# Constant products in TensorE's waits, a shorter table build, two output queues and a moved conversion schedule in a recurrence-plus-experts kernel

## The chip, the core and the metric

The kernel runs on one core of one Trainium2 chip. The core has TensorE (PE in the profile; PEld is its weight load), VectorE (DVE), ScalarE (ACT), GpSimd (POOL) and SyncE (SP), which issues transfers. ScalarE and GpSimd can issue transfers as well, each on a queue of its own. The metric is device microseconds of one execution, as the median of several runs.

## What is computed

Three stages in a row, all f32, with B=4, H=8, S=768, D=48 and 3072 tokens of width 384:

```python
for t in range(S):                               # decayed linear attention
    cur = einsum('bhd,bhe->bhde', u * k[t], v[t])
    y[t] = einsum('bhd,bhde->bhe', r[t], state + cur)
    state = w * state + einsum('bhd,bhe->bhde', k[t], v[t])
x = y.reshape(tokens, 384)
x = max(x @ w1, x @ w2, x @ w3) @ w_out          # 384 -> 768 -> 384
xn = x / sqrt(mean(x * x) + 1e-6) * rms_g
out = (silu(xn @ w_gate) * (xn @ w_val)) @ w_out2   # 384 -> 1536 -> 384
```

## The kernel before

Tokens go in 24 tiles of 128 (six chunks of time, four batches); a **unit** is the four tiles of a chunk, 512 tokens, and units are numbered from 0. The recurrence is done chunk-wise: `raw` (r and k, transposed) is multiplied by tables of powers of `w` and of their reciprocals (`qk`, made by `tables`), TensorE multiplies the two (**scores**, `pe_a`, tile `pa`), VectorE puts them under a mask into `Dg`, and TensorE forms the **output** `py` (`pe_y`) and the **state product** `pkv` (`pe_st`). `tables2` and `tables3` make another table, `kt`, which TensorE transposes (tile `pk`). ScalarE and VectorE split each output into a high and a low part, `x`.

Every large product is done as three (`mm3`, L99 to L101: high by high, high by low, low by high). In the first expert stage (`a_l1`) a unit has 18 **slots**, six blocks f by three weights w, of nine products each, and then six slots of output products (`a_out`). A slot's result `pl{unit}_{f}_{w}` takes one of four PSUM banks (`psm`) in turn; w=0 is copied out by ScalarE (`c`), w=1 and w=2 are maximised into it by VectorE, and after w=2 ScalarE casts the result to `h1h`. So slot 9 is f=3, w=0, and slot 13, f=4, w=1, takes the bank that slot 9 had. The four `psx` banks hold `pa`, `py`, `pkv` and `pk`.

Weights come as 64-bit words. A **conversion** (`tick`) of one piece is a load (`wraw`, SP), three ScalarE activations (`conv_exp`, L137 to L140), one VectorE operation a tick later, and then the split into high and low (unit 0's weights) or weight sums on VectorE and a store to HBM. It needs a `wf` buffer of six, which the store of six pieces earlier has to give back. In unit 0 ticks follow the table `U0T`; in units 1 to 4 there are nine, behind the slots n for which n % 8 is 0, 3 or 6.

The order on each engine is the order of the code: `att_steps` gives the recurrence in steps, and the loop over slots takes so many of them after each slot. Before anything else TensorE multiplies a constant by itself 24 times (`WARM`, L634). Its products are plain f32 of 128x128 by 128x128, and each leaves two records in the trace. The second expert stage (units two at a time) is not touched but for the last transfers, in `b_out`: for the last unit ScalarE or VectorE copies each finished third into SBUF, the last third in two halves, and SP transfers the four pieces (L939, L943).

Of the kernel before, what the change touches and what calls it, by code (L numbers as in the profile page):

```python
# [9 lines left out]
F32 = mybir.dt.float32  # L10
# [6 lines left out]
ALU = mybir.AluOpType  # L17
# [9 lines left out]
NRU = 8  # L27
DVE_WL = (2, 16, 19, 22)
RMS_EARLY = 2
WARM = 24  # L30
TKI = (0, 0, 2)
TKP = (1, 1, 1, 1, 1, 1)
HF = 2
# [27 lines left out]
NB = S // 128  # L61
NT = B * NB
NP = H // 2
# [3 lines left out]
def r32(ap):  # L67
    return ap.bitcast(F32)
# [3 lines left out]
def rwkv_moe_kernel(ctx, tc, rkT, rkv, wd, ub, cst, rg, w1p, wo1p, w2p, out):  # L72
    nc = tc.nc
    act, dve, pool, pe, sync = nc.scalar, nc.vector, nc.gpsimd, nc.tensor, nc.sync
# [7 lines left out]
    ap_ = sA.enter_context(tc.tile_pool(name="moea", bufs=1, side="left"))  # L82
    tp = sT.enter_context(tc.tile_pool(name="att", bufs=1, side="right"))
# [10 lines left out]
    ones = cp.tile([128, 128], F32R, name="ones")  # L94
# [3 lines left out]
    def mm3(o, lh, ll, rh, rl, start, stop, **kw):  # L98
        pe.matmul(o, lh, rh, start=start, stop=False, **kw)  # L99
        pe.matmul(o, lh, rl, start=False, stop=False, **kw)  # L100
        pe.matmul(o, ll, rh, start=False, stop=stop, **kw)  # L101
# [119 lines left out]
    def tick(n=1):  # L221
        for _ in range(n):
            i = tick_n[0]
            tick_n[0] += 1
            for off, fn in ((3, conv_load), (1, conv_exp), (0, conv_shift), (-1, conv_put)):
                if 0 <= i + off < NJ:
                    fn(i + off)
# [3 lines left out]
    ident = cp.tile([128, 128], F32, tag="wf", bufs=6, name="ident")  # L231
    cmask = csb[:, 0:128].bitcast(U32)
    m01 = csb[:, 128:129], csb[:, 130:131]
    small = tp.tile([128, 4, NP], F32, name="small")
    wsb, wcl, w128, ok = (small[:, n] for n in range(4))
    usb = tp.tile([128, DM], F32, name="usb")
    qk = tp.tile([128, 2, NP, 128], F32, name="qk")
    kt = tp.tile([128, DM], F32, name="kt")
# [22 lines left out]
        loads.append(lambda: sync.dma_start(t[:, VO:], rkv[i, :, 2 * DM:]))  # L261

    def tables():
        p = ap_.tile([128, NP, 65], F32, tag="h1h", name="ptab")
        pool.memset(p[:, :, 0:1], 1.0)
        dve.tensor_scalar(out=wcl, in0=wsb, scalar1=0.7, scalar2=1.1, op0=ALU.max, op1=ALU.min)
        dve.tensor_tensor(out=ok, in0=wsb, in1=wcl, op=ALU.is_equal)
        dve.tensor_copy(p[:, :, 1:2], wcl.unsqueeze(2))
        n = 1
        while n < 64:  # L270
            dve.tensor_tensor(out=p[:, :, n + 1:2 * n + 1], in0=p[:, :, 1:n + 1],
                              in1=p[:, :, n:n + 1].to_broadcast([128, NP, n]), op=ALU.mult)
            n *= 2
        dve.reciprocal(qk[:, 1, :, 64:128], p[:, :, 1:65])
        act.copy(qk[:, 0, :, 64:128], p[:, :, 0:64])
        act.copy(qk[:, 1, :, 0:64], p[:, :, 63::-1])
        act.copy(qk[:, 0, :, 0:64], qk[:, 1, :, 127:63:-1])
        return p

    def tables2(p):  # L280
        w64 = p[:, :, 64:65]
        dve.tensor_tensor(out=w128.unsqueeze(2), in0=w64, in1=w64, op=ALU.mult)
        R = ap_.tile([128, NP, 128], F32, tag="c1", bufs=3, name="Rtab")
        dve.tensor_tensor(out=R[:, :, 64:128], in0=qk[:, 1, :, 0:64],
                          in1=w64.to_broadcast([128, NP, 64]), op=ALU.mult)
        dve.tensor_tensor(out=R[:, :, 0:64], in0=qk[:, 1, :, 0:64],
                          in1=w128.unsqueeze(2).to_broadcast([128, NP, 64]), op=ALU.mult)
        return R

    def tables3(R):  # L290
        pk = psx.tile([128, NP, 2, 64], F32, tag="x", name="pk")
        for pr in range(NP):
            pe.transpose(pk[:, pr].rearrange("p j d -> p (j d)"), R[:, pr, :], ident)
        act.copy(kt.rearrange("p (r j d) -> p r j d", j=2, d=D), pk[:, :, :, 0:D])
# [45 lines left out]
    def prep2(i):  # L340
        if i // B < NB - 1:
            k = st[i]["tm"][:, KO:KO + DM]
            pool.tensor_tensor(out=k, in0=k, in1=kt, op=ALU.mult)

    def pe_a(i):
        s = st[i]
        raw = s["raw"]
        pa = [psx.tile([128, NP, 128], F32, tag="x", name=f"pa{i}_{j}") for j in range(2)]
        for pr in range(NP):
            for j in range(2):  # L350
                sl = slice(64 * j, 64 * j + 48)
                pe.matmul(pa[j][:, pr], raw[sl, 1, pr], raw[sl, 0, pr], start=True, stop=True)  # L352
        s["pa"] = pa
# [50 lines left out]
    def pe_y(i):  # L404
        s = st[i]
        c, b = divmod(i, B)
        tm = s["tm"]
        py = s["py"] = psx.tile([128, 3, 128], F32, tag="x", name=f"py{i}")
        lanes = []
        for n in range(4):  # L410
            lane = []
            for k in range(3):
                m = (n + TURN[k] * (i >= TURNED)) % 4
                pr, o = (k, 32 * m) if m < 3 else (3, 32 * k)
                ops = [(tm[:, VO + 144 * pr + 48 * j + o:VO + 144 * pr + 48 * j + o + 32],
                        s["Dg"][:, 2 * pr + j]) for j in range(2) if o != (64, 0)[j]]
                if c > 0:
                    ops.append((Tst[b][:, pr, o:o + 32], s["raw"][:, 0, pr]))
                for m, (l, r) in enumerate(ops):
                    lane.append((py[32 * n:32 * n + 32, k], l, r, m == 0, m == len(ops) - 1))  # L420
            lanes.append(lane)
        for m in range(max(map(len, lanes))):
            for lane in lanes:
                if m < len(lane):
                    o, l, r, start, stop = lane[m]
                    pe.matmul(o, l, r, start=start, stop=stop)  # L426
# [84 lines left out]
    def a_l1(u, f, w, o=0, n=512):  # L511
        cs = slice(o, o + n)
        xh, xl = xt[u][:, 0], xt[u][:, 1]
        if u not in hs:
            if u == NB - 1:
                t = sB["r"].tile([128, 2, F1, 512], F32R, tag="h2", name=f"h1{u}")
                hs[u] = t[:, 0], t[:, 1]
            else:
                hs[u] = [ap_.tile([128, F1, 512], F32R, tag=t, name=f"{t}{u}") for t in ("h1h", "h1l")]
        hh, hl = (t[:, f, cs] for t in hs[u])  # L520
        p = psm.tile([128, 512], F32, tag="m", name=f"pl{u}_{f}_{w}_{o}")
        wt = wts["a", f]
        for k in range(3):
            sl = slice((w * 3 + k) * 128, (w * 3 + k) * 128 + 128)
            mm3(p[:, :n], wt[:, 0, sl], wt[:, 1, sl], xh[:, k, cs], xl[:, k, cs], k == 0, k == 2)
        if w == 0:
            c1 = ap_.tile([128, 512], F32, tag="c1", bufs=3, name=f"c1{u}_{f}_{o}")
            a_l1.c1 = c1
            act.copy(c1[:, :n], p[:, :n])  # L529
        else:  # L530
            c1 = a_l1.c1
            dve.tensor_tensor(out=c1[:, :n], in0=p[:, :n], in1=c1[:, :n], op=ALU.max)  # L532
        if w == 2:
            act.copy(hh, c1[:, :n])  # L534
            later.append(lambda: (pool if n < 512 else dve).tensor_tensor(
                out=hl, in0=c1[:, :n], in1=r32(hh), op=ALU.subtract))
# [77 lines left out]
    with tc.manual_schedule():  # L614
        pool.memset(wsb, 1.0)
        dve.memset(raws[0], 0.0)
        for j in range(2):
            sync.dma_start(wsb[64 * j:64 * j + 48], wd[48 * j:48 * j + 48])
        load_tile(0)
        load_next(4)  # L620
        sync.dma_start(ident, cst[:, 0:128])
# [10 lines left out]
        pw = psm.tile([128, 512], F32, tag="m", name="pw")  # L632
        for _ in range(WARM):
            pe.matmul(pw[:, 0:128], r32(ones), r32(ones), start=True, stop=True)  # L634
        steps = list(att_steps())
        pos = 0
        tick(TKI[0])
        tb = tables()
        load_tile(1)
        load_next(4)  # L640

        prep(0)
        pe_a(0)
        tick(TKI[1])
        prep_b(0)
# [174 lines left out]
        for u in range(NB):  # L820
# [14 lines left out]
            for n, sl in enumerate(slots):  # L835
# [25 lines left out]
                if u == 0:  # L861
                    tick(U0T[n] if n < len(U0T) else 0)
                elif u < L:
                    if n % 8 in (0, 3, 6):
                        tick()
                elif u == L:
                    if n == 0:
# [62 lines left out]
        def b_out(f, d, h, po, first, last, u):  # L930
            wt = wo[f]
            o = 128 * d
            mm3(po[d], wt[:, 0, o:o + 128], wt[:, 1, o:o + 128], h[0], h[1], first, last)
            if not last:
                return
            ob = sb.pop(0) if d == 2 else br.tile([128, 512], F32, tag="ob", bufs=2, name=f"ob{u}_{d}")
            if u < NB - 1 or d < 2:
                (dve.tensor_copy if d == 1 else act.copy)(ob, po[d])
                sync.dma_start(out[u, :, d], ob)  # L939
            else:  # L940
                for eng, cs in ((act.copy, slice(0, 256)), (dve.tensor_copy, slice(256, 512))):
                    eng(ob[:, cs], po[d][:, cs])
                    sync.dma_start(out[u, :, d, cs], ob[:, cs])  # L943
            if d == 2:
                sb.append(ob)

# [53 lines left out]
        for p in range(NB // 2):  # L1000
# [84 lines left out]
            last_m, n = {}, 0  # L1085
# [11 lines left out]
            n = 0  # L1097
            for m, (_, _, kind, g, arg) in enumerate(plan):
                if kind == "M":
# [26 lines left out]
                    f = n // 10 + 2  # L1126
# [30 lines left out]
            for b in range(3 * F2 - (9 if more else 0)):  # L1157
                f, d = divmod(b, 3)
# [194 lines left out]
```

## Time and profile before

| | us |
|---|---|
| median of 3 runs (lowest, highest) | 810.82 (810.12, 811.65) |
| the profiled execution | 817.82 |
| its span, first to last instruction | 816.1 |
| TensorE busy in the span | 792.5 (97%) |
| VectorE, ScalarE, GpSimd busy | 570.2, 418.7, 210.3 |

The span is what the trace shows; the profiled execution has 1.7 us around it, and it is 0.9% longer than the median of the unprofiled runs. A busy TensorE is not one at its peak: its clock is granted at one of two levels, 1.0 (2.4 GHz) or 0.5 (1.2 GHz), and the mean over the span is 0.986. In the view of windows the clock stands behind the busy times.

### The profile page before, as it was taken

The page shows a single profiled execution, that of the slowest core. Times are in us where ns is not written, and L with a number is a line of the kernel's source. Part 1 is how long each engine was busy: PE and PEld are TensorE (multiplying, and loading weights), DVE is VectorE, ACT ScalarE, POOL GpSimd, SP SyncE. Part 2 cuts the span into 40 slices and gives each one's busy share as a digit, 9 for nine tenths or more (in the row PEclk, how much of TensorE's full clock was granted, in tenths as well). Part 3 has the DMA queues.
Part 4 walks back from the last instruction along what each step waited for, and adds up shares of the span by engine and source line. Part 5 has one row for each costly group of instructions (what it writes and reads, how often), then busy time and mean ns, then how long its engine had stood idle before and what let it go on. Part 6 is the DMA issues. An engine that isn't in the chain of part 4 may idle for free.

```text
span 816.1 us, 14059 instructions
## 1 busy us (share of the span) xinstructions
PE 792.5 (97%) x5098; PEld 654.7 (80%) x5098; DVE 570.2 (70%) x980; ACT 418.7 (51%) x780; POOL 210.3 (26%) x225
## 2 busy tenths in 40 slices
PE   6799999999999999999999999999999999999996
PEld 6688888778888888888888888788888788888884
DVE  8888859759968758518947679866677974665551
ACT  1888773444454453223577666555444555444431
POOL 2376633424325313012457673000000000000000
PEclk8889999999999999999999999999999999999998
DMA  8976775676577653226269874318454405554211
GB/s 243 262 220 202 244 223 143 217 220 196 154 243 206 196 184 104 75 86 203 87 216 345 292 237 162 129 52 278 137 182 152 124 32 173 156 155 139 74 40 43
DMA packets 83738, 139.28 MB, mean 171 GB/s; under 512 B 10566, under 2 KB 47046, under 8 KB 83660
## 3 DMA queue, kind: packets, MB, share of 16 engines
q1 hardware_dynamic: 80316, 122.37, 49.5%
q0 software_dynamic: 3200, 15.73, 5.0%
q8 instruction: 42, 0.69, 0.4%
q14 instruction: 36, 0.29, 0.1%
q10 hardware_dynamic: 144, 0.20, 0.1%
HBM read 98.65 MB, written 35.41 MB: 164 GB/s over the span
## 4 chain that ended last, share of the span: by engine, by line
PE 87%; DVE 5%; DMA 3%; ACT 2%; issue 1%; POOL 0%; SPq 0%; DVEq 0%; ACTq 0%; POOLq 0%
PE px L99 11%; PE px L100 11%; PE px L101 11%; PE pl L99 8%; PE pl L101 8%; PE pl L100 8%; PE pa L100 5%; PE pa L101 5%; PE pa L99 5%; PE py L426 4%; PE pa L352 3%; PE po L99 3%; PE po L100 3%; PE po L101 3%; PE pkv L390 1%
## 5 line engine op out<-in xcount | busy, mean ns | idle before, releaser
L99 PE MATMUL pl<-x,w_a 128*128 128x512 f32 (+1 forms) x342 | 131.9, 386 | 2.0 <-ACT c L529 1.9
L101 PE MATMUL pl<-x,w_a 128*128 128x512 f32 (+1 forms) x342 | 129.6, 379 | 1.3 <-DVE w_a L156 0.7
L100 PE MATMUL pl<-x,w_a 128*128 128x512 f32 (+1 forms) x342 | 129.5, 379 | 0.2 <-DVE x L442 0.2
L99 PEld LDWEIGHTS pl<-x,w_a 128*128 128x128 f32 x342 | 64.3, 188 | 15.7 <-ACT c L529 2.3
L532 DVE TENSOR_TENSOR c<-pl,c 128x512 f32<-128x512 f32 (+1 forms) x76 | 50.0, 657 | 37.6 <-PE pl L101 31.7
L101 PEld LDWEIGHTS pl<-x,w_a 128*128 128x128 f32 x342 | 64.3, 188 | 14.0 <-DVE w_a L156 0.9
L100 PEld LDWEIGHTS pl<-x,w_a 128*128 128x128 f32 x342 | 64.3, 188 | 11.9 <-DVE x L442 0.4
L1071 DVE TENSOR_TENSOR px<-px,sb 128x512 f32<-128x512 f32 x56 | 39.0, 699 | 33.1 <-PE px L101 31.5
L335 POOL TENSOR_SCALAR_AFFINE_SELECT Dg<-a 128x1024 f32<-128x1024 f32 x24 | 29.4, 1223 | 110.5 <-DVE a L332 83.0
L534 ACT CAST h1h<-c 128x512 fp32r<-128x512 f32 (+1 forms) x32 | 19.0, 593 | 69.5 <-DVE c L532 69.4
L1059 ACT COPY sb<-px 128x512 f32<-128x512 f32 x63 | 37.0, 587 | 32.4 <-PE px L101 28.5
L100 PE MATMUL px<-hb,wo 128*128 128x512 f32 x132 | 51.5, 391 | 0.2 <-DVE hb L1057 0.2
L695 POOL TENSOR_TENSOR ws<-wsf,ws 128x384 fp32r<-128x384 f32 x40 | 41.8, 1044 | 38.4 <-ACT ws L694 22.0
L99 PE MATMUL px<-hb,wo 128*128 128x512 f32 x132 | 51.5, 391 | 0.0
L101 PE MATMUL px<-hb,wo 128*128 128x512 f32 x132 | 51.4, 389 | 0.0
L147 DVE SCALAR_TENSOR_TENSOR wf<-wf,wraw 128x384 uint32<-128x384 uint32 x60 | 42.6, 712 | 11.1 <-ACT wraw L140 10.7
L137 ACT ACTIVATE wf<-wraw 128x384 f32<-128x384 f32 x60 | 33.3, 555 | 28.5 <-DMA w2o<-wf 12.2
L426 PE MATMUL py<-Dg,tm 128*32 128x128 f32 x768 | 41.1, 293 | 0.0
L1095 DVE TENSOR_TENSOR hb<-h,hb 128x512 fp32r<-128x512 f32 x36 | 24.9, 691 | 21.8 <-ACT hb L1094 21.6
L139 ACT ACTIVATE wraw<-wraw 128x384 uint16<-128x384 uint32 x60 | 38.8, 646 | 1.9
L140 ACT ACTIVATE wraw<-wf 128x384 f16<-128x384 f32 x60 | 38.7, 645 | 1.9
L426 PEld LDWEIGHTS py<-Dg,tm 128*32 128x32 f32 x768 | 34.4, 117 | 4.6 <-issue 3.1
(305 smaller groups left out, 2071.9 us busy)
## 6 DMA issues: line engine op xcount, KB each, us to landing
ws<-w2s SPq DMA_DIRECT2D x80, 384.0 KB, 3.1
w2s<-ws POOLq DMA_DIRECT2D x40, 384.0 KB, 3.8
wraw<-in_w2p SPq DMA_DIRECT2D x36, 384.0 KB, 5.9
raw<-in_rkT SPq DMA_DIRECT2D x48, 192.0 KB, 4.8
tm<-in_rkv SPq DMA_DIRECT2D x24, 384.0 KB, 4.4
wsf<-w2f SPq DMA_DIRECT2D x120, 64.0 KB, 3.2
tm<-in_rkv SPq DMA_DIRECT2D x24, 288.0 KB, 5.1
wraw<-in_w1p SPq DMA_DIRECT2D x18, 384.0 KB, 6.9
```

Of the source, the lines that this page charges most:

```text
L99: pe.matmul(o, lh, rh, start=start, stop=False, **kw)
L100: pe.matmul(o, lh, rl, start=False, stop=False, **kw)
L101: pe.matmul(o, ll, rh, start=False, stop=stop, **kw)
L137: act.activation(w, hi.bitcast(F32), AF.Copy, scale=2.0 ** -112)
L139: act.activation(x[:, :, 0], lo, AF.Copy, scale=2.0 ** -29 * (1 - 2.0 ** -12), bias=-0.4996)
L140: act.activation(x[:, :, 1].bitcast(F16), w, AF.Copy)
L147: dve.scalar_tensor_tensor(out=wu, in0=wu, scalar=3, in1=cbits(n).bitcast(U32), op0=ALU.logical_shift_left, op1=ALU.bitwise_or)
L426: pe.matmul(o, l, r, start=start, stop=stop)
L532: dve.tensor_tensor(out=c1[:, :n], in0=p[:, :n], in1=c1[:, :n], op=ALU.max)
L695: pool.tensor_tensor(out=t[:, :, 1], in0=r, in1=r32(t[:, :, 0]), op=ALU.subtract)
L1059: (act.copy if kind == "e" else dve.tensor_copy)(get(ks[1]), get(ks[0]))
L1071: dve.tensor_tensor(out=o, in0=a, in1=b, op=op)
```

## The change

Four edits. **Constant products:** `unread` multiplies the constant `ones` by itself into a bank that the next real product overwrites, `FILL[key]` times, ahead of the transposes (`k`), of the scores of tiles 1 to 5 (`a1` to `a5`) and of five slots of unit 0 (`l{column}_{f}_{w}`): 95 in all; `WARM` falls from 24 to 20. **Tables:** the reciprocals of 64 powers are formed as products of eight and eight (two reciprocals of 32 elements per partition and one product of 256), the clamped `w` is written straight into the table, the comparison `ok` is made later, and the two halves of `wd` are loaded by SP and ScalarE. **Last transfers:** of the last unit's four output pieces the first and the third are issued by ScalarE, the others by SP. **Conversions:** in units 1 to 4 the nine ticks stand behind slots 0, 3, 6, 9, 12, 15, 17, 19 and 21 instead of 0, 3, 6, 8, 11, 14, 16, 19 and 22.

```diff
-WARM = 24
+WARM = 20
+FILL = dict(k=18, a1=12, a2=18, l0_0_0=10, a3=5, l0_0_1=4, l0_0_2=4, l0_1_0=4, a4=7, l256_0_0=5, a5=8)
...
-        dve.tensor_scalar(out=wcl, in0=wsb, scalar1=0.7, scalar2=1.1, op0=ALU.max, op1=ALU.min)
-        dve.tensor_tensor(out=ok, in0=wsb, in1=wcl, op=ALU.is_equal)
-        dve.tensor_copy(p[:, :, 1:2], wcl.unsqueeze(2))
+        wcl = p[:, :, 1:2]
+        dve.tensor_scalar(out=wcl, in0=wsb.unsqueeze(2), scalar1=0.7, scalar2=1.1, op0=ALU.max, op1=ALU.min)
...
-        dve.reciprocal(qk[:, 1, :, 64:128], p[:, :, 1:65])
+        dve.reciprocal(low, p[:, :, 1:9])
+        dve.reciprocal(high, p[:, :, 0:57:8])
+        dve.tensor_tensor(out=qk[:, 1, :, 64:128].rearrange("p r (a b) -> p r a b", b=8),
+                          in0=low.unsqueeze(2).to_broadcast([128, NP, 8, 8]),
+                          in1=high.unsqueeze(3).to_broadcast([128, NP, 8, 8]), op=ALU.mult)
...
+        dve.tensor_tensor(out=ok.unsqueeze(2), in0=wsb.unsqueeze(2), in1=p[:, :, 1:2], op=ALU.is_equal)
...
+        unread(pk[:, 0].rearrange("p j d -> p (j d)"), "k")
...
+    def unread(t, key):
+        for _ in range(FILL.get(key, 0)):
+            pe.matmul(t, r32(ones), r32(ones), start=True, stop=True)
...
+        unread(pa[0][:, 0], f"a{i}")
...
+        if u == 0:
+            unread(p[:, 0:128], f"l{o}_{f}_{w}")
...
-            sync.dma_start(wsb[64 * j:64 * j + 48], wd[48 * j:48 * j + 48])
+            (sync, act)[j].dma_start(wsb[64 * j:64 * j + 48], wd[48 * j:48 * j + 48])
...
-                    if n % 8 in (0, 3, 6):
+                    if n in (0, 3, 6, 9, 12, 15, 17, 19, 21):
...
-                sync.dma_start(out[u, :, d], ob)
+                (act if u == NB - 1 and d == 0 else sync).dma_start(out[u, :, d], ob)
...
-                for eng, cs in ((act.copy, slice(0, 256)), (dve.tensor_copy, slice(256, 512))):
+                for eng, queue, cs in ((act.copy, act, slice(0, 256)), (dve.tensor_copy, sync, slice(256, 512))):
...
-                    sync.dma_start(out[u, :, d, cs], ob[:, cs])
+                    queue.dma_start(out[u, :, d, cs], ob[:, cs])
```

TensorE's row at the start of the program, before and then after (`pw` is the warm-up's bank; `raw_95` to `raw_97` are the inputs of tiles 0 to 2; `py` and `pkv` belong to tile 0):

```order
L634 MATMUL pw<-ones 128x128 x24
L352 MATMUL pa_0_170<-raw_95 128x128
...
L293 MATMUL pk<-ident,Rtab 128x128 x4
L352 MATMUL pa_0_216<-raw_96 128x128
...
L426 MATMUL py_228<-Dg_182,tm_104 32x128 x16
L390 MATMUL pkv_248<-tm_104 64x48 x8
L352 MATMUL pa_0_295<-raw_97 128x128
```
```order
L649 MATMUL pw<-ones 128x128 x20
L364 MATMUL pa_0_166<-raw_95 128x128
...
L354 MATMUL pk<-ones 128x128 x18
L300 MATMUL pk<-ident,Rtab 128x128 x4
L354 MATMUL pa_0_231<-ones 128x128 x12
L364 MATMUL pa_0_231<-raw_96 128x128
...
L439 MATMUL py_255<-Dg_178,tm_104 32x128 x16
L402 MATMUL pkv_275<-tm_104 64x48 x8
L354 MATMUL pa_0_322<-ones 128x128 x18
L364 MATMUL pa_0_322<-raw_97 128x128
```

Thirty constant products now stand between tile 0's and tile 1's scores, and eighteen between tile 0's state product and tile 2's scores.

ScalarE's row in unit 1, from the cast of slot 8 to the copy of slot 12, before and then after (`h1h` is that cast, `c_3_0` the copy of slot 9, `c_4_0` that of slot 12, `wf` and `wraw` the conversion, `yt` and `x` a tile's output):

```order
L534 CAST h1h_1383<-c_2_0_1636 128x512
L137 ACTIVATE wf_1707<-wraw_1527 128x384
L139 ACTIVATE wraw_1527<-wraw_1527 128x384
L140 ACTIVATE wraw_1527<-wf_1707 128x384
L529 COPY c_3_0_1722<-pl_3_0_0_1712 128x512
L441 CAST yt_1777<-py_1748 128x256
L441 CAST x_1438<-py_1748 128x128
L534 CAST h1h_1383<-c_3_0_1722 128x512
L137 ACTIVATE wf_1821<-wraw_1652 128x384
L139 ACTIVATE wraw_1652<-wraw_1652 128x384
L140 ACTIVATE wraw_1652<-wf_1821 128x384
L529 COPY c_4_0_1836<-pl_4_0_0_1826 128x512
```
```order
L549 CAST h1h_1475<-c_2_0_1728 128x512
L544 COPY c_3_0_1807<-pl_3_0_0_1797 128x512
L138 ACTIVATE wf_1812<-wraw_1619 128x384
L140 ACTIVATE wraw_1619<-wraw_1619 128x384
L141 ACTIVATE wraw_1619<-wf_1812 128x384
L454 CAST yt_1869<-py_1840 128x256
L454 CAST x_1530<-py_1840 128x128
L549 CAST h1h_1475<-c_3_0_1807 128x512
L544 COPY c_4_0_1921<-pl_4_0_0_1911 128x512
```

The copy of a slot with w=0 now stands ahead of the conversion that stood ahead of it, and the conversion ahead of the output casts.

ScalarE's row at the end of the program, before and then after (`ob` is the first third of the last unit's output, `sb` the last third):

```order
L938 COPY ob_0_7434<-px_4522 128x512
L942 COPY sb_4143<-px_4524 128x256
```
```order
L953 COPY ob_0_7526<-px_4614 128x512
L954 DMA out<-ob_0_7526 128x512
L957 COPY sb_4235<-px_4616 128x256
L958 DMA out<-sb_4235 128x256
```

Two of the four last issues moved from SP to ScalarE, each behind the copy that it sends.

## Rows read from the trace of the kernel before

**Rows 1.** Page, part 1: busy us (share of the span) x instructions, by engine.
```profile
PE 792.5 (97%) x5098; PEld 654.7 (80%) x5098; DVE 570.2 (70%) x980; ACT 418.7 (51%) x780; POOL 210.3 (26%) x225
```

**Rows 2.** Waits of TensorE, 60 to 816 us: total us, times, longest.
```profile
PE pl L99 <- ACT c L529: 1.9, 1, 1.9
PE pa L352 <- PE pa L352: 0.8, 1, 0.8
```

**Rows 3.** Windows: length, busy us (count) by engine, then clock, DMA share, GB/s.
```profile
12.50:18.50 6.00, 4.05 (x37) 3.36 (x41) 5.26 (x7) 0.48 (x1) 2.28 (x3) 0.50 1.06 307
...
53.50:56.00 2.50, 2.50 (x36) 1.98 (x28) 1.85 (x6) 2.16 (x6) 2.41 (x3) 0.50 0.06 18
...
57.00:130.00 73.00, 73.00 (x691) 60.87 (x691) 57.00 (x106) 53.56 (x101) 38.55 (x37) 1.00 0.73 223
```

**Rows 4.** Timeline, TensorE, warm-up: start us, us, engine, line, operation, tiles, count.
```profile
2.15 3.35 PE L634 MATMUL pw<-ones 128*128 128x128 f32 x14 [2.15 <-DVE ones L628]
...
5.78 3.51 PE L634 MATMUL pw<-ones 128*128 128x128 f32 x30
```

**Rows 5.** Timeline, VectorE, 4 to 15.6 us: tables and first inputs.
```profile
4.83 0.17 DVE L266 TENSOR_SCALAR small<-small 128x4 f32<-128x4 f32 x1 [0.58 <-DMA small<-in_wd]
...
5.31 1.39 DVE L271 TENSOR_TENSOR ptab<-ptab 128x4 f32<-128x4 f32 x6
...
6.74 1.75 DVE L274 RECIPROCAL qk<-ptab 128x256 f32<-128x256 f32 x1
...
9.19 0.69 DVE L314 TENSOR_TENSOR raw<-raw,qk 128x512 f32<-128x512 f32 x1
...
11.52 0.42 DVE L284 TENSOR_TENSOR Rtab<-qk,ptab 128x256 f32<-128x256 f32 x1
...
14.31 1.20 DVE L316 TENSOR_TENSOR raw<-raw,qk 128x1024 f32<-128x1024 f32 x1
```

**Rows 6.** Timeline, TensorE, 29 to 69 us: scores (L352) and slots (L99, L101).
```profile
29.50 1.25 PE L352 MATMUL pa<-raw 48*128 48x128 f32 x16 [0.48 <-PE pl L101]
...
32.72 0.39 PE L99 MATMUL pl<-x,w_a 128*128 128x256 f32 x1
...
44.18 0.39 PE L99 MATMUL pl<-x,w_a 128*128 128x256 f32 x1
...
49.55 0.28 PE L101 MATMUL pl<-x,w_a 128*128 128x256 f32 x1
...
51.28 0.92 PE L352 MATMUL pa<-raw 48*128 48x128 f32 x11 [1.45 <-issue]
...
56.75 0.39 PE L99 MATMUL pl<-x,w_a 128*128 128x256 f32 x1
...
64.28 1.16 PE L352 MATMUL pa<-raw 48*128 48x128 f32 x16
...
68.06 0.50 PE L99 MATMUL pl<-x,w_a 128*128 128x512 f32 x1
```

**Rows 7.** Chain that ended last, 14 to 40 us: start us, us, what.
```profile
22.11 7.37 DMA wraw<-in_w1p
```

**Rows 8.** Timeline, ScalarE, second unit (unit 1): a conversion and a copy.
```profile
146.70 0.54 ACT L137 ACTIVATE wf<-wraw 128x384 f32<-128x384 f32 x1 [5.50 <-DMA w2f<-wf]
...
148.44 0.55 ACT L529 COPY c<-pl 128x512 f32<-128x512 f32 x1
```

**Rows 9.** Timeline, VectorE, second unit: after the copy, and a tile's input.
```profile
149.03 0.69 DVE L532 TENSOR_TENSOR c<-pl,c 128x512 f32<-128x512 f32 x1 [5.18 <-ACT c L529]
...
164.69 1.22 DVE L316 TENSOR_TENSOR raw<-raw,qk 128x1024 f32<-128x1024 f32 x1
```

**Rows 10.** Timeline, SP queue, 808 to 816 us: the last three transfer issues.
```profile
808.38 0.33 SPq L939 DMA_DIRECT2D out<-ob  x1
808.80 1.85 SPq L943 DMA_DIRECT2D out<-sb  x1
810.75 0.44 SPq L943 DMA_DIRECT2D out<-sb  x1
```

## What I predicted before the changed kernel ran

> **What bounds the kernel now.** I read the busy shares first, then who TensorE waits for, then the clock by stretch, then the two ends of the program. TensorE is busy 97% of the span [rows 1], so only its idle time, its slow stretches and what follows its last product can be won back. After 60 us it waits only twice for longer than 0.2 us: 1.9 us for a ScalarE copy and 0.8 us for an input [rows 2]. So everything in front of 60 us is passed on to the end one for one, and those two stalls are the only gaps behind it. Before 57 us it is different: the granted clock is at 0.50, the 1.2 GHz level, in 12.5 to 18.5 and in 53.5 to 56, each time behind waits, and at 1.00, the 2.4 GHz level, from 57 us on [rows 3]. At the other end, 5.35 us pass between the start of the last transfer's issue, 810.75 [rows 10], and the end of the span, 816.1.
>
> **First unit: the price of a product of the constant.** The 24 warm-up products of before are the same shape as the 95 new ones, and each leaves two records. Fourteen records start at 2.15 and take 3.35 us; thirty later ones take 3.51 us, the last lasting 0.275 [rows 4]. So a record costs (3.51-0.275)/29 = 0.1116 us at the fast rate and about 0.213 at the slow one, a product 0.223 or 0.427. 95 products are 21.2 us at the fast rate. That is the largest number of the change, and it has to be set against the waits it is to fill.
>
> Here the Trainium skill says otherwise: its page "TensorE: Matmul & The Clock Gate", section "Back-to-back issue gap", gives about 81 ns for a matmul of 128 columns in a stream of weight loads and matmuls. By it the 95 products would be an estimate of 7.7 us and would fit into the waits. The trace shows 223 ns for this f32 product, and the trace decides.
>
> **First unit: when VectorE lets TensorE start.** The two `wd` halves now leave on two queues instead of one behind the other, so the clamp L266 at 4.83 starts some 0.4 us earlier (estimate: one issue). The flag comparison and the copy between it and L271 leave the path: L266 to L271 takes 0.48, one step of L271 is 1.39/6 = 0.23, so 0.25 goes. The reciprocal of 256 elements takes 1.75 [rows 5]; two of 32 elements lie between 0.17 (L266, four elements) and 0.39 (that plus an eighth of 1.75) each, I take 0.25, nearer to the small step since they are one; then comes one product of 256 elements like L284, 0.42. That is 0.92, so 0.8 goes. Together 1.45: L314 ends at 8.4 instead of 9.88, and the first scores can start at 8.45. The 20 warm-up products end before that (40 records, about 8.1), so four fewer cost nothing.
>
> **First unit: the sum on TensorE.** The real work from the first scores to the first slot behind the fifth tile's state, all at the fast rate: first scores 1.2; four transposes 0.45 (four records of 0.112); four tiles of scores, outputs and state product, 29.50 to 32.72 = 3.22 each, 12.88; four slots of nine products at 1.2, 4.8; 45 products from 44.18 to the end of the one at 49.55, 5.49; the fifth tile, which has state products as well, 64.28 to 68.06 = 3.78 [rows 6]. That is 28.6. With the 95 products, 8.45 + 28.6 + 21.2 = 58.25. In before the same place is reached at 56.75: **1.5 us later**, if TensorE never waits on the way. It never does: with 30 products ahead of it the second tile's scores come up at 8.45+1.2+6.7+0.45 = 16.8, while their input (L316, 14.31 plus 1.20) is now ready at about 14.2 (15.51-1.45, plus 0.15 for the comparison that moved in front of it) [rows 5]; the fifth tile's scores come up at 54.4, while in before they could start at 51.28. So the products do what they are for, the clock stays at its upper level, and the 5.47 us of the fifth tile (51.28 to 56.75) become 3.78; but they are roughly twice as long as the waits. Their surplus eats the 1.45 us of the tables and more. Ends: +0.7 (records of 0.108, slots without a start-up gap) to +2.3 (one wait of 0.8 left). The weight loads and conversions on ScalarE get more slack, not less; the chain of waits there ran over the landing of a weight transfer issued at 22.11 that took 7.37 [rows 7], and it no longer decides.
>
> **Second unit: conversions behind copies.** In before, the conversion of slot 8 stands ahead of the copy `c` of slot 9 on ScalarE. It waits 5.50 us for a DMA to give its buffer back, then takes 1.74 us, and only then, from 148.44 on, the copy frees the bank [rows 8] that slot 13 needs: the 1.9 us stall. Now the copy comes first and finds ScalarE idle from 146.70-5.50 = 141.2 on, so the bank is free 5 us before slot 13. What is queued behind the conversion is now the cast of a tile's output, which comes at about 148.5 instead of 148.90, so nothing is later. The whole 1.9 goes. The 0.8 us stall is the thirteenth tile's input, which VectorE wrote from 164.69 on after it had sat 5.18 us for the same copy [rows 9]; five weight sums also move behind it, so I take this 0.8 off too. What is late next is slot 15's bank, freed by VectorE after that cast; there I count about half a microsecond of slack. Sum **-2.7**; ends: -1.0 (part of the stall comes back at slot 15, the 0.8 stays) and -2.7, the whole of both. In units 2 to 4 there is no stall to remove. There one conversion moves ahead of the second output copy, some 1.8 us on ScalarE; the next user of that bank starts two slots and a tile pair later, over 6 us (three slots of 2.05), so it costs nothing unless its own buffer is more than 4 us late.
>
> **The end.** SP issues the last four output pieces. The second takes 0.33, the third 1.85, and the fourth can only start at 810.75 [rows 10]. With the first and third on ScalarE's queue each queue has two, the fourth is issued when its copy ends, about 809.2, that is 1.55 earlier. What follows it, 5.35 us to the end of the span, moves with it. Ends: 0, if the third issue was held by the transfers and not by its queue, and -2.0 (the third is 1.5 earlier as well). I take **-1.5**, nearer to the 0.33 that an issue behind one other costs. ScalarE's first issue falls between two copies, in a wait for TensorE.
>
> The Trainium skill speaks against this part: "DMA: Bandwidth & Descriptors", section "Issuing engines are not separate DMA queues", says that transfers of all issuing engines share the same 16 DMA engines and that several issuers save issue time only, usually little beside the transfer. By it the end would gain between nothing and the 1.5 us of that one issue, which is what the row lets it be here.
>
> **Sum.** 1.5 - 2.7 - 1.5 = -2.7 us against the profiled execution's 817.82 (span 816.1): 815.1. The median of the three runs is 810.82; in the ratio 815.1/817.82 the forecast is **808.1 us**.
>
> **Rivals.**
> 1. *The products are cheap enough to fit* (0.11 us each, one record, half of what the warm-up shows). Then the waits decide: the fifth tile starts about 0.6 earlier, as the transfer of rows 7 regains an idle gap, and saves 1.69 of clock: -2.3 instead of +1.5, in all -6.5, **804.4**. Against it stand the two records per product. The Trainium skill's price above (same page and section) would lead here too; the trace bears it out for no f32 product.
> 2. *The stall moves instead of going*: the conversion that still waits for its buffer holds the output cast, and slot 15 stands. Then -0.5 instead of -2.7, in all -0.5, **810.3**. Against: the cast is not later than before.
> 3. *The tail keeps its length*: the shared engines held the third issue. Then 1.5 - 2.7 = -1.2, **809.6**. For it: two whole pieces are on their way when the third is issued; against: no issue behind one other took more than 0.44 there.
> 4. *Slower: the clock falls all the same.* If products run at the lower level, each costs 0.2 more. The 48 products ahead of the second and third tile stand where before the clock was at 0.50 [rows 3]; all of them slow would be +9.8, in all +7.1, **817.9**. It decides from 22 slow products on (4.3 us, from -2.7 to +1.6). Against: in my sum TensorE has no wait there, and each fall in before comes behind one.
>
> **How the numbers follow.** 0.2% is 1.6 us, about what a measurement of this kernel tells from no change. Forecast 0.55 (of it 0.45 beyond that bound, 0.10 within, as +2.3 or -2.0 in its terms brings it under), rival 1 0.14, rival 2 0.12, rival 3 0.11, rival 4 0.08. Faster 0.45+0.14+0.05 (rivals 2 and 3 with the other terms at their better ends) = 0.64; within 0.27; slower 0.09, rival 4 and a hundredth for rivals 2 and 3 together. The range goes from rival 1's 804.4 to 811.0, which takes in rivals 2 and 3 with the first unit at its +2.3; what is left out is rival 4 and the far side of rival 1.
>
> **What would show it.** Clock 1.00 from 10 to 57 us and no TensorE wait over 0.3 us there; the second tile's scores at 16 to 17 us and the slot behind the fifth tile at about 58; 95 products with 190 records at 0.112. No wait of TensorE for `c` near 148; ScalarE's copy before its conversion's wait. The last issue at about 809.2 less what the rest moves, and 5 to 6 us from it to the end. I am wrong if the slot behind the fifth tile starts before 56 (rival 1), if the clock shows 0.50 there (rival 4), or if a wait over 1 us stands in 140 to 170.

## The result

The changed kernel is slower: 816.38 us, the median of 7 executions (815.62 to 819.24), against 811.41 for the kernel before (7 executions, 810.12 to 814.43). The ratio is 1.0065, 95% interval 1.0053 to 1.0078, so about 5 us. The prediction said 808.1, and its range ended at 811.0.

The two profiled executions alone say the opposite: 816.38 us now (span 814.7), 817.82 before (span 816.1). That contradiction is the key to this case. The profile after has the page's busy shares

```profile
PE 804.5 (99%) x5280; PEld 669.0 (82%) x5280; DVE 565.8 (69%) x981; ACT 420.8 (52%) x780; POOL 212.8 (26%) x225
```

12 us more of busy TensorE than in [rows 1]. Its waits, first those of 0 to 60 us, then those behind (total, times, longest), are

```profile
PE pw L649 <- DVE ones L643: 2.1, 1, 2.1
...
PE px L100 <- DVE px L1086: 0.7, 1, 0.7
```

so apart from the program's very start the view shows no wait of TensorE in the first unit, and both stalls of [rows 2] are gone. Of the 95 constant products the groups by line, 0 to 60 us, show 190 records (busy us, mean ns, idle before), and TensorE's timeline gives their place:

```profile
L354 PE MATMUL pa<-ones 128*128 128x128 f32 x100 | 12.1, 276 | 0.0
...
L354 PE MATMUL pl<-ones 128*128 128x128 f32 x54 | 7.0, 278 | 0.0
...
L354 PE MATMUL pk<-ones 128*128 128x128 f32 x36 | 4.3, 278 | 0.0
```
```profile
9.00 1.16 PE L364 MATMUL pa<-raw 48*128 48x128 f32 x16
10.09 4.29 PE L354 MATMUL pk<-ones 128*128 128x128 f32 x36
14.22 0.60 PE L300 MATMUL pk<-ident,Rtab 128*128 128x128 f32 x4
...
17.43 1.16 PE L364 MATMUL pa<-raw 48*128 48x128 f32 x16
...
24.77 1.16 PE L364 MATMUL pa<-raw 48*128 48x128 f32 x16
...
54.87 1.16 PE L364 MATMUL pa<-raw 48*128 48x128 f32 x16
...
58.65 0.39 PE L100 MATMUL pl<-x,w_a 128*128 128x256 f32 x1
```

These answer to [rows 4, 6]. The place to which the prediction made its sum is the first slot behind what it calls the fifth tile; by the numbers that start at 0 this is tile 5, and so it is called from here on (its "second tile" is tile 1). That slot starts at 58.65 (forecast 58.25). From 10.09 to 14.22 eighteen products pass, 0.229 each.

### The profile page after: what moved, and what is told of

Read it like the earlier page. It is cut to its first block, busy times and chain, and to the rows that moved or that the text cites. A ratio compares the mean times of both kernels' runs of the same rounds, so it can differ in the third digit from the quotient of the medians.

```text
span 814.7 us, 14431 instructions
## 1 busy us (share of the span) xinstructions
PE 804.5 (99%) x5280; PEld 669.0 (82%) x5280; DVE 565.8 (69%) x981; ACT 420.8 (52%) x780; POOL 212.8 (26%) x225
## 4 chain that ended last, share of the span: by engine, by line
PE 97%; DVE 1%; ACT 0%; issue 0%
PE px L100 11%; PE px L101 11%; PE px L102 11%; PE pl L100 10%; PE pl L101 9%; PE pl L102 9%; PE pa L101 5%; PE pa L102 5%; PE pa L100 5%; PE py L439 5%; PE po L100 3%; PE pa L364 3%; PE po L102 3%; PE po L101 3%; PE pkv L402 1%; PE pa L354 1%
## 5 line engine op out<-in xcount | busy, mean ns | idle before, releaser
L101 PE MATMUL pl<-x,w_a 128*128 128x512 f32 (+1 forms) x342 | 129.4, 378 | 0.0
L101 PEld LDWEIGHTS pl<-x,w_a 128*128 128x128 f32 x342 | 64.3, 188 | 11.5
L101 PE MATMUL px<-hb,wo 128*128 128x512 f32 x132 | 51.6, 391 | 0.2 <-DVE hb L1072 0.2
L439 PE MATMUL py<-Dg,tm 128*32 128x128 f32 x768 | 37.9, 275 | 0.0
L371 DVE COPY_PREDICATED Dg<-csb,pa 128x512 f32<-128x512 uint32 x48 | 31.8, 727 | 5.8 <-PE pa L364 3.6
```

## Experiments

One table for all profiles. "Slot" is the start of the first slot behind tile 5, "middle" the time from there to the end of TensorE's last product, "end" from that to the end of the span; all three are differences of times in the profiled execution. "Before" in the ratio is the kernel before, run on the same chip in the same session.

| kernel | median, us | ratio to before (95%) | profiled: us | slot | middle | end |
|---|---|---|---|---|---|---|
| before, the profile of the prediction | 811.41 | | 817.82 | 56.75 | 751.55 | 7.8 |
| changed | 816.38 | 1.0065 (1.0053, 1.0078) | 816.38 | 58.65 | 749.16 | 6.9 |
| b_again: before | 811.25 | 0.9993 (0.9983, 1.0002) | 810.98 | 52.99 | 748.73 | 7.6 |
| b_fill: products alone | 818.54 | 1.0084 (1.0067, 1.0100) | 816.90 | 58.98 | 748.70 | 7.5 |
| b_tab: tables alone | 811.22 | 1.0000 (0.9989, 1.0011) | 810.74 | 52.64 | 748.75 | 7.6 |
| b_conv: conversions alone | 811.18 | 0.9989 (0.9978, 1.0000) | 812.48 | 53.70 | 749.34 | 7.8 |
| b_tail: last transfers alone | 810.36 | 0.9990 (0.9979, 1.0001) | 809.31 | 52.33 | 748.72 | 6.6 |
| a_nofill: changed, no products | 809.66 | 0.9982 (0.9970, 0.9994) | 813.12 | 55.92 | 748.85 | 6.6 |
| a_nofill2: the same again | (one) | | 809.37 | 51.24 | 748.79 | 7.7 |
| a_few: 21 products | 811.47 | 0.9993 (0.9979, 1.0008) | 811.17 | 53.44 | 749.29 | 6.8 |
| a_half: 46 products | 810.17 | 0.9985 (0.9972, 0.9999) | 811.98 | 54.01 | 749.33 | 7.0 |
| a_early: first 48 products | 813.14 | 1.0017 (1.0004, 1.0031) | 811.38 | 53.92 | 748.76 | 7.0 |
| a_late: last 47 products | 814.24 | 1.0039 (1.0025, 1.0053) | 813.93 | 56.95 | 748.73 | 6.5 |

**b_again: is the profiled execution a typical one?** No edit.

> The kernel before, unchanged, looked at again. Theory A (in most executions the clock of the first unit falls for less than in the one profiled before, so the waits there cost some 7 us less): the executions lie around 811 us, spans around 809.5, and a profile of such a one shows a mean clock above 0.99 and the first slot behind the fifth tile some 5 us or more ahead of 56.75. Rival B (the executions are alike, and the profiled one merely lost some time everywhere): clock 0.986 again, the slot at 56 to 57, and the difference of 7 us spread over the whole span or behind 60 us. Rival C (this chip is another one): all executions move together, to 817.

It is not typical. In 82 further executions of the kernel before, in three sessions, none took longer than 814.72; 817.82 lies above all of them. The second profile took 810.98. Its clock is as low as the first one's (0.987 against 0.986), so that part of theory A fell: the clock falls here as well. What differs stands in three places. The slot behind tile 5 starts 3.76 earlier (5 or more was expected), the middle is 2.82 shorter, the end 0.2. The middle first: TensorE's waits behind 60 us, and ScalarE's row that answers to [rows 8].

```profile
PE pa L352 <- PE pl L101: 0.2, 1, 0.2
PE pa L100 <- DVE hb L1057: 0.2, 1, 0.2
PE px L100 <- DVE hb L1057: 0.2, 1, 0.2
```
```profile
139.18 0.57 ACT L137 ACTIVATE wf<-wraw 128x384 f32<-128x384 f32 x1 [5.54 <-DMA w2f<-wf]
139.78 0.66 ACT L139 ACTIVATE wraw<-wraw 128x384 uint16<-128x384 uint32 x1
140.47 0.64 ACT L140 ACTIVATE wraw<-wf 128x384 f16<-128x384 f32 x1
140.98 0.56 ACT L529 COPY c<-pl 128x512 f32<-128x512 f32 x1
```

The conversion waits for its buffer here too, 5.54 us, but the buffer comes back at 139.18, not at 146.70, and the copy is in time. Both stalls, 1.9 and 0.8, are missing, as they are in b_fill, b_tab and b_tail below, which also have the old places of the conversions (middles of 748.7). The order of the code allows the stalls; four of the five profiles with that order don't have them.

The first unit: windows of ten us of this execution (length; busy us of PE, PEld, DVE, ACT, POOL; clock, DMA share, GB/s), and then TensorE's tile 5.

```profile
10.00:20.00 10.00, 6.78 (x73) 5.50 (x74) 8.50 (x13) 0.60 (x2) 4.98 (x4) 0.68 1.07 287
20.00:30.00 10.00, 7.62 (x89) 6.42 (x87) 8.35 (x13) 9.28 (x20) 3.22 (x3) 0.67 0.96 267
30.00:40.00 10.00, 10.00 (x121) 8.87 (x123) 9.93 (x15) 9.74 (x21) 5.87 (x5) 0.79 1.06 301
40.00:50.00 10.00, 8.64 (x107) 7.97 (x97) 8.91 (x13) 9.44 (x23) 8.07 (x8) 1.00 1.05 298
50.00:60.00 10.00, 10.00 (x123) 8.98 (x120) 8.52 (x15) 9.04 (x18) 8.12 (x9) 1.00 0.72 220
```
```profile
49.12 1.25 PE L352 MATMUL pa<-raw 48*128 48x128 f32 x16 [1.02 <-issue]
...
52.99 0.39 PE L99 MATMUL pl<-x,w_a 128*128 128x256 f32 x1
```

Tile 5 starts at 49.12, 2.16 ahead of [rows 6], and takes 3.87 instead of 5.47: here the clock is at 1.00 from 40 us on, and there it is at 0.50 once more in 53.5 to 56 [rows 3].

**a_nofill, a_nofill2, b_fill: the products.** In b_fill the two lines below and the calls of `unread` are added to before; a_nofill takes the products out of the changed kernel.

```diff
-WARM = 24
+WARM = 20
+FILL = dict(k=18, a1=12, a2=18, l0_0_0=10, a3=5, l0_0_1=4, l0_0_2=4, l0_1_0=4, a4=7, l256_0_0=5, a5=8)
```
```diff
-WARM = 20
-FILL = dict(k=18, a1=12, a2=18, l0_0_0=10, a3=5, l0_0_1=4, l0_0_2=4, l0_1_0=4, a4=7, l256_0_0=5, a5=8)
+WARM = 24
+FILL = {}
```

> The kernel before with the 95 constant products and 20 warm-up products as its only change. Theory A: the changed kernel's 816.4 plus what its other parts save, 2.7 + 1.4 + up to 1.5, so 820.5 to 822. Rival B: at or below 811.4, since the products keep the clock up.

> The changed kernel with no constant products and with 24 warm-up products; tables, conversions and last transfers as changed. Theory A: 811.4 less 2.7 for the conversions, 1.4 for the end and 0 to 1.5 for the tables, so 805.8 to 807.3. Rival B (one of the other three parts is what costs time): 815 or more. If the constant products cost or give nothing: 816.4.

> The version without constant products once more, for a second profile: its executions spread from 808.6 to 813.1, and the first profile was the slowest of them. If the spread lies in the first unit: an execution under 810 has its slot behind the fifth tile at 52 to 53 instead of 55.92, the same 748.7 to 749.3 us from there to the last product, and a shorter wait for the x of ScalarE than 2.9.

The products cost about 7 us: b_fill is 7.0 above before, a_nofill 6.7 below the changed kernel (both figures take in the four warm-up products that differ). That the clock stays up (0.998 in b_fill's profile) does not make up for that. b_fill came out 2 lower and a_nofill 2.4 higher than expected, and one reason fits both: the other three edits together are worth about 2, not 4 to 5.6. Rival B is out.

The two profiles of a_nofill differ by 4.68 at the slot (55.92 and 51.24; 52 to 53 was expected of the second), and by less than 0.1 in the middle, as expected. The second was taken on another chip, but the twelve executions on one chip already go from 808.6 to 813.1. ScalarE's waits in 19 to 52 us, first of the longer execution, then of the shorter one (its only line), then of the kernel before in the prediction's profile:

```profile
ACT wf L138 <- DMA wraw<-in_w1p: 4.6, 4, 2.0
```
```profile
ACT h1h L549 <- DVE c L547: 0.4, 1, 0.4
```
```profile
ACT wf L137 <- DMA wraw<-in_w1p: 1.9, 2, 1.7
```

The chain that ended last in the longer one (start, us, what) goes through two transfers where the shorter one's goes through conversions:

```profile
19.81 8.43 DMA tm<-in_rkv
28.30 10.19 DMA wraw<-in_w1p
```
```profile
19.83 0.45 ACT wf L138
20.30 0.64 ACT wraw L140
20.97 0.64 ACT wraw L141
```

When weights arrive in time, ScalarE's conversions stand one behind the other, and the chain of waits runs through them from 19 to 38 us. Late weights lengthen that row by the waits for them. Three of the four waits here, 3.9 of the 4.6, lie ahead of the place where the chain leaves ScalarE. With the 0.24 by which its row starts later (18.73 and 18.49) they make up the 4.1 by which the next products on the chain come late (47.04 and 42.95); another 0.5 is a longer gap ahead of tile 5's scores (1.59 and 1.04). In the prediction's profile [rows 7] the waits for weights are 1.9, in b_again the view shows none, and tile 5 was 2.16 late. So without the products the chain of the first unit runs through ScalarE's row and the weights from 19 to about 40 us. It isn't free of TensorE: ahead of 19 us it runs through TensorE's products, at a clock of 0.50 from 15 to 17.5 in both profiles of a_nofill, and in b_tab it does so again in 27.7 to 35 (0.50 up to 34).

**a_half, a_few, a_early, a_late: how many products, and where.** The counts of the changed kernel are replaced by, in this order,

```diff
+FILL = dict(k=9, a1=6, a2=9, l0_0_0=5, a3=2, l0_0_1=2, l0_0_2=2, l0_1_0=2, a4=3, l256_0_0=2, a5=4)
...
+FILL = dict(k=9, a1=6, a2=6)
...
+FILL = dict(k=18, a1=12, a2=18)
...
+FILL = dict(l0_0_0=10, a3=5, l0_0_1=4, l0_0_2=4, l0_1_0=4, a4=7, l256_0_0=5, a5=8)
```

> The changed kernel with about half as many constant products (46: k 9, a1 6, a2 9, and so on). Theory A: between the version without them and the changed kernel; if the products simply add to the path, 49 x 0.223 = 10.9 us would come off, but the waits come back, so 805 to 809. If the number of products does not matter as long as there are some: 816.

> The changed kernel with 21 constant products, sized by the waits of the version without them (2.4, 1.4 and 1.7 us ahead of the transposes and of the second and third tile's scores, 0.223 each: k 9, a1 6, a2 6), none later. If the clock's fall in the first unit lies in time that the transfers leave over anyway: the same as without products, 809.7. If the fall between 14 and 18 us is on the path: 1 to 1.5 faster than without, 808.5.

> The changed kernel with only the 48 constant products of its first three places (k 18, a1 12, a2 18), none behind the third tile's scores. Theory A, as it stands now: these push the third tile's scores from about 22.2 to 24.8, but the inputs of the later tiles come by transfers that set the fifth tile at 49 to 51 whatever TensorE did before, so nearly all of the delay is taken back by waits: 809 to 811, like the version without products. Rival: the early delay also holds up the loads behind it, and the fifth tile moves with it: 812 to 813.

> The changed kernel with only the 47 constant products of its later places (l0_0_0, a3, l0_0_1, l0_0_2, l0_1_0, a4, l256_0_0, a5). Theory A: third tile's scores at about 22.2, and from there the row of work and products of the changed kernel without a wait, 33.9 us to the slot behind the fifth tile: slot at 56 instead of 58.65, 813 to 814. Rival (late products lie in waits too): 809 to 811.

a_half: its products take 10.5 us (46 x 0.229) and at 810.17 it is not clearly slower than a_nofill (0.5 in the medians); they fit into waits. Expected were 805 to 809; a_nofill itself has no execution below 808.6. a_half's clock is 1.00 throughout the first unit, and a_few's mean is 0.996; neither is faster than a_nofill, whose profiles have 0.989 and 0.993. Their profiles show a gain from the higher clock and where it goes: ScalarE gets tile 1's output at 17.05 in a_few and at 17.42 in a_half, against 18.73 and 18.49 without products, and then waits 3.5 and 3.7 us for weights. In a_few:

```profile
17.05 0.48 ACT L454 CAST x<-py 128x384 fp32r<-128x384 f32 x1 [3.55 <-PE py L439]
...
24.07 0.55 ACT L138 ACTIVATE wf<-wraw 128x384 f32<-128x384 f32 x1 [2.15 <-DMA wraw<-in_w1p]
```

That this is so in most executions is not shown. a_few came out 1.8 above the expected 809.7, with executions from 808.47 to 813.41; its interval against before overlaps a_nofill's, so "the same" and "2 us slower" can't be told apart; a gain from the clock in the median it does not show.

a_late did nearly what was expected of it (814.24 for 813 to 814, the slot at 56.95 for 56). From 27 us on the view shows no wait of TensorE; the scores of tile 2 still have a gap ahead of them, those of tiles 3 and 5 have none:

```profile
21.41 1.45 PE L364 MATMUL pa<-raw 48*128 48x128 f32 x16 [1.74 <-issue]
...
30.81 1.16 PE L364 MATMUL pa<-raw 48*128 48x128 f32 x16
...
53.17 1.16 PE L364 MATMUL pa<-raw 48*128 48x128 f32 x16
...
56.95 0.39 PE L100 MATMUL pl<-x,w_a 128*128 128x256 f32 x1
```

a_early went the rival's way, 813.1 where 809 to 811 was expected. Its profile is of one of its fastest executions, and there ScalarE gets tile 1's output at 19.58 (18.49 in a_nofill2) and waits 1.4 us for weights; tile 5 comes at 50.05 instead of 47.37. So in this execution the early surplus isn't taken back in full: it delays ScalarE's row. Why half of its executions take 813.6 to 815.4 stays open, since no trace shows one.

**b_conv: the conversions.**

```diff
-                    if n % 8 in (0, 3, 6):
+                    if n in (0, 3, 6, 9, 12, 15, 17, 19, 21):
```

> The kernel before with the conversions' new places in units 1 to 4 as its only change. The second look at before had neither the 1.9 nor the 0.8 us stall of unit 1, so in most executions there is nothing to take away: 811.5, within 0.3. If the stalls stand in most executions and that look was the exception: 2.7 faster, 808.8.

0.75 below before in the medians, interval 0 to 1.8: it may take the stalls out of the executions that have them, but 2.7 in most executions is excluded. In the profile the middle is 749.34, no shorter than b_again's. In the table the eight profiles with the new places have middles of 748.73 to 749.34, and the old places have 748.70 to 748.75 in all but the prediction's profile.

**b_tail: the last transfers.**

```diff
-                sync.dma_start(out[u, :, d], ob)
+                (act if u == NB - 1 and d == 0 else sync).dma_start(out[u, :, d], ob)
...
-                for eng, cs in ((act.copy, slice(0, 256)), (dve.tensor_copy, slice(256, 512))):
+                for eng, queue, cs in ((act.copy, act, slice(0, 256)), (dve.tensor_copy, sync, slice(256, 512))):
...
-                    sync.dma_start(out[u, :, d, cs], ob[:, cs])
+                    queue.dma_start(out[u, :, d, cs], ob[:, cs])
```

> The kernel before with the last transfers on two queues as its only change. From the profiles of before and of the changed kernel, end of the last product to end of the span, 7.6 to 6.9: 0.6 to 0.9 faster, 810.6 to 810.9, with the last issue beginning 0.9 after the last product and the transfer behind it longer than 5.35. The prediction's term was 1.5 (810.0); its rival 3 was 0 (811.5).

1.1 in the medians (interval -0.1 to 1.7), 1.0 in the profiles' ends against b_again (7.6 to 6.6). Over all profiles the end is 7.5 to 7.8 with one queue (five profiles, mean 7.65), and with two it is 6.5 to 7.0 in seven (mean 6.8) and 7.7 in one, a_nofill2. With two queues the end goes with the length of the last issue: 0.76 to 0.80 us in the two profiles with the shortest ends, 1.24 and 1.30 in those with 7.0, 1.81 in the one with 7.7 (only a_nofill, with an issue of 0.38 and an end of 6.6, lies off this line). SP's two issues in b_tail:

```profile
801.12 0.33 SPq L939 DMA_DIRECT2D out<-ob  x1
801.94 0.80 SPq L943 DMA_DIRECT2D out<-sb  x1
```

**b_tab: the tables.** All of the changed kernel but the products, the conversions and the last transfers (their lines as in before, `WARM` 24).

```diff
-        dve.reciprocal(qk[:, 1, :, 64:128], p[:, :, 1:65])
+        dve.reciprocal(low, p[:, :, 1:9])
+        dve.reciprocal(high, p[:, :, 0:57:8])
```

> The kernel before with the tables by 16 reciprocals and the two wd loads on two queues as its only change. First inputs 0.8 earlier than in before (the rest of the 1.45 is taken by a wait for the transfer of raw). If it is passed on down the chain of inputs: 0.7 to 0.9 faster, 810.6. If the transfers of the first unit decide and swallow it: 811.4.

No gain is shown, and none of 0.7 is excluded: the ratio is 1.0000, and its interval goes down to 0.9989, which is 0.9 us. The profile passes part of the gain on: tile 1's scores start at 14.36 against b_again's 14.99, the slot at 52.64 against 52.99. The view shows no wait of ScalarE for weights in 19 to 52 us in either, so the expected reason, transfers that swallow the gain, isn't seen here. Of the first tile's part b_tab says nothing: its 24 warm-up products hold the first scores until 9.88, though their input is ready at 8.59.

## Why the prediction was wrong

**The step that failed** is the one before the forecast: "in the ratio 815.1/817.82 the forecast is 808.1 us". It treats the 7.0 us between the profiled execution and the median as if they were spread evenly over the program. Against b_again's execution they lay in three places: 3.76 ahead of tile 5's slot, 2.82 in the middle, 0.2 at the end. The first two are the waits, and the fall of the clock behind them, that the change was to remove. So the forecast took credit for them and then took the same 7 us off once more. Against an execution without them the terms are others: the first unit costs 5.7 (b_again to the changed kernel) and not 1.5, and the second unit gives nothing clear instead of 2.7. The sum itself, 815.1 for one execution, missed the 816.38 by 1.3: 0.4 at the slot, 0.3 in the middle, 0.6 at the end. It could come that near because a sum without waits doesn't depend on how long the waits of one execution were. The table ahead of the prediction held the warning: 817.82 lies 6 us above the highest of three executions that agree within 1.6, and the two stalls and the transfer of 7.37 us [rows 2, 7] go back to waits for transfers, which the second profile has at other lengths or not at all.

**First unit.** The price of a product was nearly right: forecast 0.223, measured 0.229. So were the absence of waits and the clock at 1.00. That the slot came within 0.4 of the sum (58.25, measured 58.65) is in part luck: the start was 0.55 late (8.45, measured 9.00), the products took 0.6 more, and the real work behind the start 0.7 less than the 28.6 counted. The late start is the warm-up. Its last record ended at 9.07, while the 8.1 of the prediction is where, by [rows 4], the last one would start; TensorE's windows from 5 to 7 us count 14 warm-up records after and 20 before, with a granted clock of 1.00 in both. But "in before the same place is reached at 56.75" holds for that one execution. In b_again, b_tab, b_conv and b_tail it is reached at 52.3 to 53.7. The sentence "the 5.47 us of the fifth tile become 3.78" counted as the products' gain what b_again has without them (3.87). On the price of a product, the Trainium skill, "TensorE: Matmul & The Clock Gate", "Back-to-back issue gap", gives about 81 ns for a matmul of 128 columns in a stream of weight loads and matmuls; 36 records of the trace, 10.09 to 14.22, make it 229 ns for this f32 product.

**VectorE's start.** Against the prediction's profile nearly all of the 1.45 came: the operation that was L314 ends at 8.53 (forecast 8.4, before 9.88). Against b_again, where it ends at 9.30, about half did. VectorE's timeline after, to be read beside [rows 5]:

```profile
4.31 1.39 DVE L272 TENSOR_TENSOR ptab<-ptab 128x4 f32<-128x4 f32 x6
5.62 0.35 DVE L275 RECIPROCAL ptab<-ptab 128x32 f32<-128x32 f32 x1
5.88 0.29 DVE L276 RECIPROCAL ptab<-ptab 128x32 f32<-128x32 f32 x1
6.21 0.42 DVE L277 TENSOR_TENSOR qk<-ptab 128x256 f32<-128x256 f32 x1
7.23 0.69 DVE L320 TENSOR_TENSOR raw<-raw,qk 128x512 f32<-128x512 f32 x1 [0.60 <-DMA raw<-in_rkT]
7.84 0.69 DVE L321 TENSOR_TENSOR raw<-raw,qk 128x512 f32<-128x512 f32 x1
```

The table itself is made as forecast: from 5.62 the three operations end at 6.63, and 0.35, 0.29 and 0.42 are close to the 0.25, 0.25 and 0.42 taken. But then VectorE waits 0.60 for `raw`, a wait that before was hidden behind the long reciprocal. And the start in the prediction's profile, the clamp at 4.83 behind a wait for `wd`, wasn't typical either: in b_again it is at 4.25 without one. What is left, some 0.8, shows in no median (b_tab). In the profiles a third of a us of it reaches the slot, both in b_tab against b_again and in the changed kernel against b_fill: there the first scores wait for VectorE until 9.33, here they start at 9.00 behind the warm-up, and the slots (58.98 and 58.65) differ by the same 0.33.

**Second unit.** The mechanism is there. ScalarE's timeline after, to be read beside [rows 8]: the copy of slot 9 is done before the conversion waits, and slot 13 finds its bank free.

```profile
139.41 0.59 ACT L544 COPY c<-pl 128x512 f32<-128x512 f32 x1 [0.59 <-PE pl L102]
142.67 0.62 ACT L138 ACTIVATE wf<-wraw 128x384 f32<-128x384 f32 x1 [2.68 <-DMA w2f<-wf]
143.32 0.67 ACT L140 ACTIVATE wraw<-wraw 128x384 uint16<-128x384 uint32 x1
144.02 0.64 ACT L141 ACTIVATE wraw<-wf 128x384 f16<-128x384 f32 x1
```

The size is what failed: the two stalls are 2.7 in one execution, and b_conv measures 0 to 1.8 in the median, with no profile of the old places but that one that has a stall to remove.

**The end.** The term was 1.5; it measured 0.8 on the means of the ends (five profiles against all eight). ScalarE's and SP's issues after (to be read beside [rows 10]):

```profile
807.10 0.36 ACTq L954 DMA_DIRECT2D out<-ob  x1
...
808.25 0.35 ACTq L958 DMA_DIRECT2D out<-sb  x1
```
```profile
807.88 0.33 SPq L954 DMA_DIRECT2D out<-ob  x1
808.70 1.14 SPq L958 DMA_DIRECT2D out<-sb  x1
```

The last issue starts 0.89 after the last product instead of 2.45: 1.56 earlier, as worked out. "What follows it moves with it" is the part that failed: from its start to the end of the span it is now 6.0 instead of 5.35. The busy share of the DMA engines in 40 slices of 798 to 820 us bears on why, first in the prediction's profile of before, then after:

```profile
DMA  0000000000000100000977117700000000000000
```
```profile
DMA  0001000000010000009896530000000000000000
```

Before, the last two pieces had the engines to themselves after two nearly empty slices; now all four go out in one piece of work, and the issue of the last one takes 1.14, not 0.44. That the last piece queues behind the others fits this, and fits the ends that grow with that issue (b_tail), but it is argued. It is half of rival 3, and it agrees with the section of the Trainium skill that the prediction set against this part ("DMA: Bandwidth & Descriptors", "Issuing engines are not separate DMA queues"), by which transfers of all issuers share the same 16 engines and only issue time is saved: the last issue came 1.56 earlier, the end 0.8.

**Rivals.** Rival 1 (cheap products) is out by their price. Rival 2 (the stall moves) did not happen, nor did rival 4: the clock stayed at 1.00 in the first unit of both profiles with all the products. The slower outcome came by a mechanism that stood under no rival: the products were right in price and place, but the waits that they were priced against are mostly shorter. In 0 to 60 us, the program's start aside, TensorE's waits add up to 10.4 us in the prediction's profile and to 6.9 to 8.6 in those of b_again, b_tab, b_conv and b_tail.

In all, against b_again's execution: +5.7 at the slot, +0.4 in the middle, -0.7 at the end, 5.4 in the span, and 5.0 in the medians.

## What to carry to other kernels

When the profiled execution lies outside the range of the timed ones, find out where its surplus lies before anything is priced: a second profile of the same kernel settles it, and until then every wait for a transfer in it is worth anything from nothing to its length. Work that nobody reads, put into TensorE's waits, paid in none of the kernels here, though the mean clock was higher with it: 46 products spread over the first unit cost nothing clear, 95 of 0.229 cost 7 us, and the kernel without them has the lowest median of all that ran, 0.9982 of before, though not clearly below those of a_half, b_conv and b_tail. A second issue queue saved the blocked issue (1.56 us) and, since the transfers behind it took longer, half of that at the end.

## What was not expected of the hardware

The time of one program varies with its waits for transfers: a_nofill's executions go from 808.6 to 813.1 us, and between its two profiles 3.9 of the 4.68 us at the slot are ScalarE's waits for weights. a_late, whose TensorE shows no wait in the first unit from 27 us on, stays within 813.9 to 814.5 in six executions. And a lower mean clock did not mean a slower program: before ran at 0.987 in 811.0 us, the changed kernel at 0.999 in 816.4.
